# Convolution with per-token taps, then a two-layer SoLU network: other first loads, weights on two queues, and a new table of step priorities

## The chip, the core and the metric

The kernel runs on one core of a Trainium2 chip. The metric is device time in microseconds (us) of one execution. The five engines of the core are named as the profile names them: PE is TensorE (matmuls), DVE is VectorE, ACT is ScalarE, POOL is GpSimd, and SP is SyncE, which issues most of the DMAs. Each engine works through its own instructions in the order in which they were built; between engines they wait for each other with semaphores. A DMA is issued from an engine's queue (here SP's, after the change also ACT's) and moved by 16 DMA engines.

## The reference

Eight sequences of 4160 tokens of 192 channels pass through two stages. Cut to what is computed:

```python
w = softmax(weight_gen, axis=-1)              # 8 heads x 7 taps for every token
x_pad = concatenate([zeros(B, 6, D), x])      # six zero rows ahead of each sequence
out[s, h, :] = sum_k w[s, h, k] * x_pad[s + k, h, :]     # 24 channels a head
h = out @ w_in                                # 33280 x 192 times 192 x 1024
solu = h * softmax(h)
ln = (solu - mean) / sqrt(var + 1e-6) * g_ln
return ln @ w_out                             # 1024 x 192
```

Each token needs the six rows ahead of it in its own sequence; the first rows of a sequence need zeros there. The weights `w_in`, `w_out` and `g_ln`: the two matrices arrive as 64-bit floats, which the kernel reads as pairs of 32-bit integers and converts on the chip.

## The kernel before

The 33280 tokens are cut into 128 runs of 260 consecutive tokens, one run to a partition, 16 runs to a sequence. A "tile" t is the t-th token of all 128 runs, so there are 260 tiles. The tiles come in chunks (4, 8, 8 and then 16 tiles) for the loads and the softmax of the taps, and in groups of 4 (the first two groups have 2) for the convolution.

**First loads.** For chunk 0, `load_x(0)` needs the six rows ahead of each run. Those of run p are the last six rows of run p-1, except where a sequence begins (partitions 0, 16, 32, ...), where they are zeros. Before, one DMA brings them for partitions 1 to 127 at once (L78), wrongly also for the sequence starts, and a third DMA then writes zeros over these eight partitions from a small tile (L80). It has to wait until the first one has landed. All loads are issued from SP's queue in the order of the program: taps of chunk 0 (`load_w(0)`, L96), the last 64 rows of `w_in` (L152, tile `raw_b`, which the profile calls `hl` after its buffer), `load_x(0)` (L78 to L80), the first 128 rows of `w_in` in two halves (L168, `raw_a`), the taps of chunk 1, `w_out` (L173, `raw_2`, shown as `raw`), `g_ln` (L177), and `load_x(1)`. Each DMA reports its end through one of eight counters, which the program takes in turn (DMAHW0 to DMAHW7); a DMA that gets a counter again waits until the one that had it before has landed.

**Convolution.** POOL multiplies a group's rows by the taps (L133) and adds the seven products in two steps (L139, L141, into one of two `half` buffers). DVE does the last addition (L366, step `fin`, tile `a`), ACT copies some columns (L372, `dup`). The softmax of a chunk's taps is seven steps `t0` to `t6` on DVE (L112, L120, L124), POOL (L114, L126) and ACT (L118, L122).

**Network.** For each pair of tiles PE transposes (`xT`, L383) and ACT and DVE split the result into a high and a low part. For each tile then: the first product into one of three PSUM buffers `h` (`mm1`, L422 and L427), the negative maximum on DVE (`max`, L441), the exponential on ACT (`exp`, L454), SoLU on DVE (`solu`, L460), the sum of squares on ACT (`sq`, L466), the high half of the result on ACT (`hi`, L473), the low half on DVE (`lo`, L477), a DMA transpose (`tr`, L485), the second product into the single PSUM buffer `po` (`mm2`, L529), and the scaling by ACT (`out`, L540). The next `mm2` waits for this `out`, and a new `mm1` waits until the `sq` and `lo` of three tiles earlier have freed its buffer.

**Weights.** The conversion runs in seven parts of three steps: `b`, `a0`, `a1` for `w_in` (512 columns each, L194 to L213) and `c0` to `c3` for `w_out` (384 columns each). They use the PSUM buffers of `h` as scratch, so the first products wait for some of them.

**What sets the order.** `issue_order` is a planner that runs when the kernel is built. It has a table of steps with an assumed cost, an engine and what each step waits for, and plays them through: whenever an engine is free it takes, of the steps that could start, the one with the lowest `t + URGENCY[name]`. The order in which the steps start in this play is the order in which they are written to the engines' queues. `URGENCY` is a table of 90 numbers.

Of the kernel before, what the change touches and what calls it, by code (L numbers as in the profile page):

```python
# [26 lines left out]
def tile_kernel(ctx: ExitStack, tc: tile.TileContext, x, weight_gen, w_in, w_out, g_ln, out):  # L27
    nc = tc.nc
# [38 lines left out]
    def load_x(c, part=0):  # L67
        t0, n = starts[c], starts[c + 1] - starts[c]
        if part == 0:
            xs[c] = io.tile([P, (TC + HALO) * D], F32, name="xt")  # L70
        xt = xs[c]
        xv = xt.rearrange("p (t d) -> p t d", d=D)
        if c == 0:

            nc.gpsimd.memset(xt[:1, : HALO * D], 0.0)
# [2 lines left out]
            nc.sync.dma_start(xv[1:, :HALO, :], x_run[: P - 1, RUN - HALO :, :])  # L78
            nc.sync.dma_start(xv[:, HALO : HALO + n, :], x_run[:, :n, :])
            nc.sync.dma_start(  # L80
                xv[::PB, :HALO, :], zeros.unsqueeze(1).broadcast_to([B, HALO, D])
            )
# [82 lines left out]

    raw_a = att.tile([P, 2 * FF], I32, name="raw_a", bufs=1)
    for f in range(2):
        nc.sync.dma_start(  # L168
            raw_a[:, f * FF : (f + 1) * FF], w_in[:P, f * FF : (f + 1) * FF]
        )  # L170
    load_w(1)
    raw_2 = att.tile([P, 2 * NJ * D], I32, name="raw_2", bufs=1)
    nc.sync.dma_start(  # L173
        raw_2.rearrange("p (j d) -> p j d", j=NJ), w_out.rearrange("(j p) d -> p j d", p=P)
    )
    g = const.tile([P, NJ], F32, name="g")
    nc.sync.dma_start(g, g_ln.rearrange("(j p) -> p j", p=P))  # L177
    load_x(1)
# [81 lines left out]
    def scale_and_sum(f, step):  # L260
# [24 lines left out]
    def prepare_second(step, half=None):  # L285
# [307 lines left out]
    f5=-90.9, f6=-122.6, f7=-80.2, fin=-1.8, hi=21.6, lo=-147.6, lw=-22, lx0=-1.4, lx1=-11.2,
    lx2=-124.2, lx3=169.4, max=5.1, mm1=26.4, mm2=33.4, od=-130.9, out=-6, p30=-16.2, p31=3.9,
    p4=42.9, p5=103.1, p6=5.8, p70=-62.9, p71=0.3, p80=126.7, p81=-54.7, q00=-14.5, q01=-183.5,
    q02=-5.9, q10=-13.7, q11=-25.1, q12=-13.9, q20=-2.5, q21=-143.1, q22=-168.3, q30=-15.9,
    q31=149.2, q32=-18.4, solu=-21.3, sq=207.5, t0=45.9, t1=-70.9, t2=79, t3=26.5, t4=120.9,
    t5=135.7, t6=73.4, tr=65.6, vb=-74.8, vr=-11.3, xT=25.4, xhi=-202.9, xld=-11.7, xlo=-60.8,
    xn=7.8,
# [243 lines left out]
```

## Time and profile before

| | |
|---|---|
| time, median of 3 runs (lowest to highest) | 1389.33 us (1389.17 to 1389.57) |
| the profiled execution | 1389.4 us |
| its span, first to last instruction | 1387.5 us |
| busy: PE, DVE, ACT, POOL | 1259.2, 1230.0, 1128.5, 1247.0 us |
| granted clock of TensorE, mean | 0.991 |
| POOL's first multiplication of a group starts, its last addition ends | 31.59 us, 1288.46 us |

The span is counted from the first instruction; the remaining 1.9 us of the execution lie around it. In the timeline a row has the start, the duration, the engine, the source line, the operation and its tiles, and in brackets how long the engine had been idle and what released it; `SPq` rows are the issuing of a DMA, not its transfer. A row of stretches has the limits, the length, then the busy time of PE, weight loads, DVE, ACT and POOL with their counts, the granted clock, the busy share of the 16 DMA engines, and GB/s.

### The profile page before, as it was taken

The numbers are of one execution on the slowest core, as the hardware profiler recorded it, in microseconds if no ns is written. First come the engines' busy times: TensorE is split into PE (matmuls) and PEld (weight loads), VectorE is DVE, ScalarE is ACT, GpSimd is POOL, SyncE is SP. The second block draws the span as 40 slices with busy tenths as digits, with TensorE's granted clock in tenths as the row PEclk, the third lists the DMA queues.
The fourth block names the chain that finished last, engine by engine and source line by source line (L and its number), as shares of the span: only waits on it lengthen the run. The fifth ranks groups of instructions, "written<-read, shape, count | busy, mean of one in ns | idle before, by whom it ended". The sixth has DMA issues, their size and how long they took to land.

```text
span 1387.5 us, 26562 instructions
## 1 busy us (share of the span) xinstructions
PE 1259.2 (91%) x10028; PEld 988.6 (71%) x10028; DVE 1230.0 (89%) x2068; ACT 1128.5 (81%) x2231; POOL 1247.0 (90%) x243
## 2 busy tenths in 40 slices
PE   0389899999999999989989999999999999999997
PEld 0267677777777777767767677777777777777776
DVE  2999898999989899889989898989899889999984
ACT  1588887888888888888888888888788888888885
POOL 1999999999999999999999999999999999999100
PEclk9989999999999999999999999999999999999999
DMA  3469768696968789697857768687858668766765
GB/s 90 139 142 194 147 128 201 124 207 122 194 130 174 146 145 195 122 198 123 186 130 166 158 149 186 118 190 145 193 109 191 146 140 176 132 133 117 134 131 116
DMA packets 565241, 210.43 MB, mean 152 GB/s; under 512 B 544329, under 2 KB 545785, under 8 KB 565112
## 3 DMA queue, kind: packets, MB, share of 16 engines
q1 hardware_dynamic: 565112, 208.73, 72.5%
q8 instruction: 79, 1.29, 0.4%
q14 instruction: 50, 0.41, 0.1%
HBM read 46.19 MB, written 25.56 MB: 52 GB/s over the span
## 4 chain that ended last, share of the span: by engine, by line
POOL 51%; DVE 16%; issue 13%; ACT 13%; PE 4%; DMA 3%; SPq 0%; POOLq 0%; DVEq 0%; ACTq 0%
POOL pr L133 27%; POOL pr L139 15%; POOL half L141 6%; DVE h L460 5%; ACT hl L473 4%; DVE hl L477 4%; ACT e L466 3%; DVE stats L441 3%; ACT e L454 3%; DVE a L366 3%; DMA xt<-in_x_dram 2%; POOL wt L114 2%; PE po L529 2%; POOL wt L126 1%; PE h L422 1%
## 5 line engine op out<-in xcount | busy, mean ns | idle before, releaser
L133 POOL TENSOR_TENSOR pr<-xt,wt 128x5376 f32<-128x5376 f32 (+1 forms) x66 | 631.3, 9565 | 23.1 <-DMA xt<-zeros 20.5
L529 PE MATMUL po<-w_hl,hlT 128*128 128x192 f16 x6192 | 558.5, 247 | 26.6 <-ACT ot L540 26.2
L529 PEld LDWEIGHTS <-hlT 128*128 128x128 f16 x6240 | 515.2, 98 | 82.2 <-issue 79.2
L477 DVE SCALAR_TENSOR_TENSOR hl<-h,hl 128x1024 f16<-128x1024 f32 x260 | 315.4, 1220 | 44.2 <-ACT e L466 31.5
L460 DVE SCALAR_TENSOR_TENSOR h<-h,stats,e 128x1024 f32<-128x1024 f32 x260 | 334.7, 1288 | 22.4 <-ACT e L454 9.2
L473 ACT ACTIVATE hl<-h 128x1024 f16<-128x1024 f32 x260 | 267.3, 1028 | 92.3 <-DVE stats L497 57.4
L139 POOL TENSOR_TENSOR pr<-pr 128x2304 f32<-128x2304 f32 (+1 forms) x66 | 332.7, 5041 | 5.2
L441 DVE TENSOR_REDUCE stats<-h 128x1 f32<-128x1024 f32 x260 | 316.1, 1216 | 8.9 <-PE h L427 8.1
L454 ACT ACTIVATE e<-h,stats 128x1024 f32<-128x1024 f32 x260 | 292.6, 1126 | 31.1 <-DVE stats L441 27.2
L466 ACT ACTIVATE e<-h,stats 128x1024 f32<-128x1024 f32 x260 | 292.3, 1125 | 5.9 <-DVE hl L477 5.4
L422 PE MATMUL h<-wa_hi,x_hi 128*128 128x512 f32 x520 | 225.4, 433 | 36.3 <-ACT e L466 22.8
L141 POOL TENSOR_TENSOR half<-pr 128x1536 f32<-128x1536 f32 (+1 forms) x66 | 225.8, 3422 | 5.2
L422 PE MATMUL h<-wa_hi,x_lo 128*128 128x512 f32 x520 | 207.5, 399 | 0.8 <-ACT x_lo L405 0.8
L422 PE MATMUL h<-wa_lo,x_hi 128*128 128x512 f32 x520 | 206.3, 397 | 0.0
L422 PEld LDWEIGHTS h<-wa_hi,x_hi 128*128 128x128 f32 x520 | 98.9, 190 | 59.3 <-ACT e L466 26.0
L427 PE MATMUL h<-wb_hi,x_hi 64*128 64x512 f32 x520 | 131.1, 500 | 0.0
L383 PE MATMUL pa<-ident,a 128*128 128x128 f32 x520 | 84.6, 286 | 44.2 <-DVE a L366 44.1
L540 ACT ACTIVATE ot<-po,stats 128x192 f32<-128x192 f32 x258 | 111.4, 432 | 8.5 <-PE po L529 8.5
L366 DVE TENSOR_REDUCE a<-half 128x768 f32<-128x1536 f32 (+1 forms) x66 | 116.4, 1764 | 1.6 <-POOL half L141 1.6
L427 PEld LDWEIGHTS h<-wb_hi,x_hi 64*128 64x128 f32 x520 | 48.6, 184 | 96.7 <-issue 96.7
L422 PEld LDWEIGHTS h<-wa_hi,x_lo 128*128 128x128 f32 x520 | 98.6, 190 | 24.3 <-ACT x_lo L405 1.6
L383 PEld LDWEIGHTS pa<-ident,a 128*128 128x128 f32 x520 | 55.8, 142 | 79.7 <-DVE a L366 44.1
(79 smaller groups left out, 1194.1 us busy)
## 6 DMA issues: line engine op xcount, KB each, us to landing
out_dram<-ot SPq DMA_DIRECT2D x65, 384.0 KB, 3.3
xt<-in_x_dram SPq DMA_DIRECT2D x30, 576.0 KB, 4.7
xt<-in_x_dram SPq DMA_DIRECT2D x30, 480.0 KB, 4.7
wt<-in_weight_gen_dram SPq DMA_DIRECT2D x15, 448.0 KB, 4.1
hlT<-hl SPq DMA_TRANSPOSE x260, 4.5
raw<-in_moe_w_out_dram SPq DMA_DIRECT2D x1, 1536.0 KB, 9.4
xt<-in_x_dram SPq DMA_DIRECT2D x3, 384.0 KB, 6.0
raw_a<-in_moe_w_in_dram SPq DMA_DIRECT2D x2, 512.0 KB, 11.5
```

The source lines that it names most:

```text
L133: nc.gpsimd.tensor_tensor(out=window(pr, 0, [(TG * D, K), (HG, n * H), (1, HG)]), in0=window(xt, t * D, [(D, K), (HG, n * H), (1, HG)]), i ...
L139: nc.gpsimd.tensor_tensor(out=pr[:, :3], in0=pr[:, :3], in1=pr[:, 3:6], op=ALU.add)
L141: nc.gpsimd.tensor_tensor(out=half, in0=window(pr, 0, [(2 * TG * D, 2), (D, n), (1, D)]), in1=window(pr, TG * D, [(5 * TG * D, 2), (D, n), ...
L422: nc.tensor.matmul(h[:, fs], lhs[:, 0, :], rhs[:, fs], start=n == 0, stop=False)
L427: nc.tensor.matmul(h[:, fs], lhs[rows, 1, :], rhs[rows], start=False, stop=n == 2,)
L441: nc.vector.tensor_reduce(stat(t, NMAX), h_of[t], axis=AX.X, op=ALU.max, negate=True)
L454: nc.scalar.activation(e, h_of[t], AF.Exp, bias=stat(t, NMAX), accum_out=stat(t, Z))
L460: nc.vector.scalar_tensor_tensor(out=h, in0=h, scalar=stat(t, SIGMA), in1=e, op0=ALU.mult, op1=ALU.mult, accum_out=stat(t, M))
L466: nc.scalar.activation(e_of.pop(t), h_of[t], AF.Square, bias=stat(t, M), scale=-float(FF), accum_out=stat(t, Q),)
L473: nc.scalar.activation(hl[:, 0, :], h_of[t], AF.Copy, scale=2.0**14)
L477: nc.vector.scalar_tensor_tensor(out=hl[:, 1, :], in0=h_of[t], scalar=2.0**14, in1=hl[:, 0, :], op0=ALU.mult, op1=ALU.subtract,)
L529: nc.tensor.matmul(po[:, :D], hlT[:, half * NJ + j, :], w2_hl[:, j, w, :], start=n == 0, stop=n == len(terms) - 1,)
```

## The change

Four things change.

1. `load_x(0)`: POOL zeroes the six rows ahead on all 128 partitions first. Then eight DMAs, one for each sequence, load the rows for the 15 partitions behind its first one, the odd ones from SP's queue and the even ones from ACT's. The DMA that wrote zeros, and its tile, are gone.
2. The loads are issued in another order: `load_x(0)` directly after the first taps, and `raw_a`, the second half of `w_out` and `g_ln` from ACT's queue. All stand ahead of ACT's first work.
3. Two scratch tiles get a pool of their own (`frac` instead of a buffer of `e`), and the sums of squares of the second weights (`second["total"]`) take the upper half of the `po` buffer instead of `pa`.
4. The planner gets another `URGENCY` table, other assumed costs for some steps (POOL's convolution 14990 + 3510 ns instead of 14206 + 3380, for example), the part `a0` ahead of `b`, and a wait of the first scaling steps for `a02` and `a12`. No instruction of a tile is added or removed by this; they are put in another order.

```diff
-            nc.gpsimd.memset(xt[:1, : HALO * D], 0.0)
-            zeros = const.tile([B, D], F32, name="zeros")
-            nc.gpsimd.memset(zeros, 0.0)
-            nc.sync.dma_start(xv[1:, :HALO, :], x_run[: P - 1, RUN - HALO :, :])
+            nc.gpsimd.memset(xt[:, : HALO * D], 0.0)
             nc.sync.dma_start(xv[:, HALO : HALO + n, :], x_run[:, :n, :])
-            nc.sync.dma_start(
-                xv[::PB, :HALO, :], zeros.unsqueeze(1).broadcast_to([B, HALO, D])
-            )
+            for b in range(B):
+                queue = nc.sync if b % 2 else nc.scalar
+                queue.dma_start(
+                    xv[b * PB + 1 : (b + 1) * PB, :HALO, :],
+                    x_run[b * PB : (b + 1) * PB - 1, RUN - HALO :, :],
+                )
...
     load_w(0)
     w_in = w_in.bitcast(I32)
     w_out = w_out.bitcast(I32)
+    load_x(0)
+    raw_a = att.tile([P, 2 * FF], I32, name="raw_a", bufs=1)
 
     raw_b = big.tile([P, FF], I32, name="hl", bufs=3)
     for f in range(2):
+        nc.scalar.dma_start(raw_a[:, f * FF : (f + 1) * FF], w_in[:P, f * FF : (f + 1) * FF])
         nc.sync.dma_start(raw_b[f * D2 : (f + 1) * D2, :], w_in[P:, f * FF : (f + 1) * FF])
-    load_x(0)
+    load_w(1)
+    raw_2 = att.tile([P, 2 * NJ * D], I32, name="raw_2", bufs=1)
+    raw_2v = raw_2.rearrange("p (j d) -> p j d", j=NJ)
+    for n in range(2):
+        js = slice(n * NJ // 2, (n + 1) * NJ // 2)
+        (nc.scalar if n else nc.sync).dma_start(
+            raw_2v[:, js], w_out.rearrange("(j p) d -> p j d", p=P)[:, js]
+        )
+    g = const.tile([P, NJ], F32, name="g")
+    nc.scalar.dma_start(g, g_ln.rearrange("(j p) -> p j", p=P))
+    load_x(1)
...
-            frac = big.tile([P, FF], F32, name="e")[:, :n]
+            frac = big.tile([P, FH], F32, name="frac")[:, :n]
...
-            second["total"] = ps_a.tile([P, 512], F32, name="pa")
+            second["total"] = second["sums"][:, 256:]
...
-    c01=19.2, c02=4.8, c10=-143, c11=7.6, c12=1.7, c20=-15.4, c21=6.6, c22=-4.8, c30=-11.2,
-    c31=-125.2, c32=78.7, dup=-17.9, exp=66.3, f0=73.9, f1=1.2, f2=-140.6, f3=-73.6, f4=-146.4,
+    c31=12.4, c32=-106.7, dup=8.7, exp=-126.7, f0=126.6, f1=-167.6, f2=7.7, f3=-16.5, f4=2.1,
+    f5=-0.2, f6=-129.7, f7=-140.1, fin=-6.2, hi=27.1, lo=-2, lw=157.1, lx0=-8.4, lx1=-95.6,
...
-        add("attA", t, POOL, 14206 if full else 7302, *after, ready=21100 if c == 1 else 0)
-        add("attB", t, POOL, 3380 if full else 1764, ("attA", t), ("fin", groups[i - 2] if i > 1 else -1))
+        add("attA", t, POOL, 14990 if full else 7500, *after, ready=15000 if c == 1 else 9000)
+        add("attB", t, POOL, 3510 if full else 1800, ("attA", t), ("fin", groups[i - 2] if i > 1 else -1))
...
-        add("mm1", t, PE, 2300, low_of(t), ("sq", t - 3), ("lo", t - 3), *after)
+        add("mm1", t, PE, 2460, low_of(t), ("sq", t - 3), ("lo", t - 3), *after)
```

What this makes of the engines' queues is shown at three places. The first is the start of SP's queue before the change, with the counter that each DMA has to wait for (`Pool` is POOL's own counter; `raw_107` is the tile of `w_out`):

```order
L96 DMA wt<-in_weight_gen_dram 128x224
L152 DMA hl<-in_moe_w_in_dram 64x1024 x2
L78 DMA xt<-in_x_dram 127x1152
L79 DMA xt<-in_x_dram 128x768
L168 DMA raw_a<-in_moe_w_in_dram 128x1024
L80 DMA xt<-zeros 8x6x192 [waits DMAHW3_49,Pool_49]
L168 DMA raw_a<-in_moe_w_in_dram 128x1024
L96 DMA wt<-in_weight_gen_dram 128x448 [waits DMAHW0_49]
L173 DMA raw_107<-in_moe_w_out_dram 128x8x384 [waits DMAHW1_49]
L177 DMA g<-in_moe_g_ln_dram 128x8x1 [waits DMAHW2_49]
L85 DMA xt<-in_x_dram 128x1536
```

DMAHW3 is the counter of the load of L78, so everything below L80 stands behind that load. After the change SP's queue begins so:

```order
L96 DMA wt<-in_weight_gen_dram 128x224
L76 DMA xt<-in_x_dram 128x768
L79 DMA xt<-in_x_dram 15x1152 [waits Pool_49]
L79 DMA xt<-in_x_dram 15x1152 x2
L79 DMA xt<-in_x_dram 15x1152 [waits DMAHW1_49]
L155 DMA hl<-in_moe_w_in_dram 64x1024 [waits DMAHW3_49]
L155 DMA hl<-in_moe_w_in_dram 64x1024 [waits DMAHW5_49]
L96 DMA wt<-in_weight_gen_dram 128x448 [waits DMAHW7_49]
L161 DMA raw_101<-in_moe_w_out_dram 128x4x384 [waits DMAHW0_49]
L85 DMA xt<-in_x_dram 128x1536 [waits DMAHW2_49]
```

No DMA waits for a load of 127 rows any more, but nearly each waits for a counter. DMAHW0 belongs first to the taps of chunk 0, DMAHW1 to the load of L76, and DMAHW2 to DMAHW7 to the first six of the eight small loads. The start of ACT's queue after the change (before, its first two rows were the table load and the conversion that is L200 here):

```order
L56 ACT_TABLE_LOAD
L79 DMA xt<-in_x_dram 15x1152 [waits Pool_49]
L79 DMA xt<-in_x_dram 15x1152 x2
L79 DMA xt<-in_x_dram 15x1152 [waits DMAHW0_49]
L154 DMA raw_a<-in_moe_w_in_dram 128x1024 [waits DMAHW2_49]
L154 DMA raw_a<-in_moe_w_in_dram 128x1024 [waits DMAHW4_49]
L161 DMA raw_101<-in_moe_w_out_dram 128x4x384 [waits DMAHW6_49]
L165 DMA g<-in_moe_g_ln_dram 128x8x1 [waits DMAHW1_49]
L118 ACTIVATE wt<-wt 128x224 [waits Pool_49]
L200 ACTIVATE h<-h 128x512 [waits DVE_49]
```

The taps of chunk 0 (L118) now stand behind eight DMAs, the last of which waits for DMAHW1, whose second owner is the eighth small load. The second place is DVE's queue up to the division of the taps of chunk 0 (L124), after the change:

```order
L112 TENSOR_REDUCE wm<-wt 128x32 [waits DMAHW0_49]
L177 TENSOR_SCALAR minus<-ident 128x128 [waits Pool_49]
L193 TENSOR_SCALAR h<-raw_a 128x512 [waits DMAHW2_49]
L196 TENSOR_SCALAR h<-raw_a 128x512 [waits DVE_49]
L198 TENSOR_SCALAR h<-h 128x512 [waits DVE_49]
L193 TENSOR_SCALAR h<-hl 128x512 [waits DMAHW5_49,DMAHW3_49]
L196 TENSOR_SCALAR h<-hl 128x512 [waits DVE_49]
L120 TENSOR_REDUCE wm<-wt 128x32 [waits Activation_49]
L198 TENSOR_SCALAR h<-h 128x512 [waits DVE_49]
L112 TENSOR_REDUCE wm<-wt 128x64 [waits DMAHW7_49]
L124 RECIPROCAL wy<-wy 128x32 [waits Activation_49]
```

Before, the first conversion of `raw_b` (`hl`) stood directly behind the maximum of the taps, and the two tap steps of L120 and L124 ahead of any step on `raw_a`. The third place is the end of the convolution on DVE, the last addition of the last group (`a<-half`, tiles 256 to 259). Before:

```order
L441 TENSOR_REDUCE stats<-h 128x1
L477 SCALAR_TENSOR_TENSOR hl<-h,hl 128x1024
L445 TENSOR_REDUCE stats<-stats 128x1
L412 TENSOR_TENSOR x_lo<-pa,x_hi 128x512
L450 RECIPROCAL stats<-stats 128x1
L366 TENSOR_REDUCE a<-half 128x4x192
L497 TENSOR_REDUCE stats<-stats 128x4
L460 SCALAR_TENSOR_TENSOR h,stats<-h,stats,e 128x1024
```

Now (lines are one lower):

```order
L440 TENSOR_REDUCE stats<-h 128x1
L476 SCALAR_TENSOR_TENSOR hl<-h,hl 128x1024
L444 TENSOR_REDUCE stats<-stats 128x1
L496 TENSOR_REDUCE stats<-stats 128x4
L365 TENSOR_REDUCE a<-half 128x4x192
L496 TENSOR_REDUCE stats<-stats 128x4
L449 RECIPROCAL stats<-stats 128x1
L459 SCALAR_TENSOR_TENSOR h,stats<-h,stats,e 128x1024
```

The neighbours are alike; what moved is the place. In DVE's queue before, 244 of the 260 `solu` steps stand ahead of this last addition and 16 behind it; now 249 stand ahead and 11 behind. At the addition for the group that begins with tile 52 it was 48 and is 49, at tile 152 it was 144 and is 148.

More of the change, by code (lines that the diff above doesn't have):

```diff
@@ L164, in tile_kernel @@
     nc.vector.tensor_scalar_mul(minus, ident, -1.0)
[L166 to L178, printed above, removed]
     for step in range(TAP_STEPS):
@@ L278, in scale_and_sum @@
         elif step == 2:
-            junk = big.tile([P, FF], F32, name="e")
+            junk = big.tile([P, FH], F32, name="frac")
             nc.scalar.activation(
@@ L588 @@
 URGENCY = dict(
-    a00=-79.4, a01=-110.4, a02=-10.4, a03=-9.5, a04=28.3, a10=35.2, a11=8.2, a12=-10.4, a13=2,
-    a14=-26.4, attA=14.7, attB=-118.7, b0=12.5, b1=28.4, b2=-7.8, b3=-40.9, b4=125.7, c00=120.1,
-    c01=19.2, c02=4.8, c10=-143, c11=7.6, c12=1.7, c20=-15.4, c21=6.6, c22=-4.8, c30=-11.2,
-    c31=-125.2, c32=78.7, dup=-17.9, exp=66.3, f0=73.9, f1=1.2, f2=-140.6, f3=-73.6, f4=-146.4,
[L593 to L599, printed above, removed]
+    a00=146.3, a01=114, a02=105.5, a03=52.4, a04=58.5, a10=-4.3, a11=-0.8, a12=-8.4, a13=73.8,
+    a14=25.5, attA=-2.8, attB=-19.6, b0=129.4, b1=-57.8, b2=-0.3, b3=52.7, b4=-112.9, c00=44.6,
+    c01=2.8, c02=-91.1, c10=-93.1, c11=-37.1, c12=-89.4, c20=-34.5, c21=-4.7, c22=16.6, c30=-144.9,
+    c31=12.4, c32=-106.7, dup=8.7, exp=-126.7, f0=126.6, f1=-167.6, f2=7.7, f3=-16.5, f4=2.1,
+    f5=-0.2, f6=-129.7, f7=-140.1, fin=-6.2, hi=27.1, lo=-2, lw=157.1, lx0=-8.4, lx1=-95.6,
+    lx2=125.7, lx3=8.5, max=40, mm1=26.6, mm2=33.6, od=-17.4, out=4.8, p30=-113.1, p31=-64.5,
+    p4=-117.2, p5=143.6, p6=-0.8, p70=179.3, p71=-15.2, p80=-6.7, p81=15.1, q00=3.8, q01=-15.7,
+    q02=16.8, q10=-99.3, q11=-14.1, q12=5, q20=-108.4, q21=-65.1, q22=0.2, q30=110, q31=144.7,
+    q32=51.3, solu=-130.8, sq=374, t0=10.4, t1=3.2, t2=84, t3=121.1, t4=-15.6, t5=26.9, t6=2.8,
+    tr=-113, vb=-142.7, vr=-62.5, xT=24.7, xhi=-12, xld=-20.5, xlo=3.7, xn=-4.4,
 )
@@ L620, in once @@
         add(name, 0, engine, cost, *((x, 0) for x in after), ready=ready)
-    parts = ["b", "a0", "a1", *(f"c{f}" for f in range(4))]
+    parts = ["a0", "b", "a1", *(f"c{f}" for f in range(4))]
     for n, part in enumerate(parts):
         w_in, size = n < 3, 512 if n < 3 else 384
-        at = (5600, 9000, 10600)[n] if w_in else 16200
+        at = (9000, 10500, 12000)[n] if w_in else 15000
         before = () if w_in else (f"{parts[n - 3]}4" if n < 6 else "q00",)
@@ L637, in issue_order @@
             f = n - 3
-            once(f"q{f}0", ACT, 700, part + "2")
+            once(f"q{f}0", ACT, 700, part + "2", "a02", "a12")
             once(f"q{f}1", PE, 660, f"q{f}0", *([f"q{f - 1}1"] if f else []))
@@ L704, in issue_order @@
     for t in range(0, run, 2):
-        add("xT", t, PE, 600, ("dup", group_of[t]), low_of(t - 2))
+        add("xT", t, PE, 500, ("dup", group_of[t]), low_of(t - 2))
         add("xhi", t, ACT, 478, ("xT", t), ("mm1", t - 3))
         if on_vector(t):
-            add("xld", t, DVE, 560, ("xhi", t), ("mm1", t - 3))
+            add("xld", t, DVE, 600, ("xhi", t), ("mm1", t - 3))
         else:
@@ L719, in issue_order @@
             after.append(("p80" if t == 3 else "p81", 0))
-        add("mm1", t, PE, 2300, low_of(t), ("sq", t - 3), ("lo", t - 3), *after)
-        add("max", t, DVE, 1131, ("mm1", t), ("exp", t - 4))
+        add("mm1", t, PE, 2460, low_of(t), ("sq", t - 3), ("lo", t - 3), *after)
+        add("max", t, DVE, 1140, ("mm1", t), ("exp", t - 4))
         add("vb", t, DVE, 70, ("max", t), ("f7", stats_of[t - 24] if t >= 24 else -1))
@@ L724, in issue_order @@
         add("exp", t, ACT, 1091, ("max", t), ("sq", t - 2))
-        add("solu", t, DVE, 1210, ("exp", t), ("vr", t))
+        add("solu", t, DVE, 1290, ("exp", t), ("vr", t))
         add("sq", t, ACT, 1091, ("solu", t))
-        add("hi", t, ACT, 904, ("solu", t), ("tr", t - 3))
+        add("hi", t, ACT, 920, ("solu", t), ("tr", t - 3))
         add("lo", t, DVE, 1135, ("hi", t))
@@ L734, in issue_order @@
             after.append(("out", t - 1))
-        add("mm2", t, PE, 2200, ("tr", t), *after)
+        add("mm2", t, PE, 2170, ("tr", t), *after)
         add("out", t, ACT, 304, ("mm2", t), ("f7", stats_of[t]), ("od", t // 4 * 4 - 5))
```

4 lines of the change are left out of this document (2 added, 2 removed).

## The prediction

> **What bounds the kernel now.** I read the page first, then the busy time by stretches, cut where POOL's convolution begins and ends.
>
> ```profile
> span 1387.5 us, 26562 instructions
> POOL 51%; DVE 16%; issue 13%; ACT 13%; PE 4%; DMA 3%; SPq 0%; POOLq 0%; DVEq 0%; ACTq 0%
> ...
> 0.00:31.59 31.59, 0.00 (x0) 0.00 (x0) 4.01 (x9) 2.97 (x5) 3.10 (x11) 1.00 0.25 74
> 31.59:1288.50 1256.91, 1168.95 (x9264) 915.15 (x9265) 1153.87 (x1933) 1052.67 (x2081) 1243.85 (x232) 0.99 0.75 156
> 1288.50:1387.50 99.00, 90.21 (x767) 73.44 (x765) 72.15 (x128) 72.85 (x147) 0.00 (x0) 0.98 0.65 124
> ```
>
> There are three stages. In the first 31.59 us no engine does more than 4 us of work. In the second POOL is busy 1243.85 of 1256.91 us, which is all but the gaps between its instructions; the chain of waits goes half through POOL. In the last 99 us POOL has nothing left and PE works off a backlog. Next, what fills the first stage, from the timeline:
>
> ```profile
> 2.46 0.48 SPq L78 DMA_DIRECT2D xt<-in_x_dram  x1
> 2.99 9.88 SPq L79 DMA_DIRECT2D xt<-in_x_dram  x1
> 12.92 1.37 SPq L168 DMA_DIRECT2D raw_a<-in_moe_w_in_dram  x1
> 28.82 0.75 SPq L80 DMA_DIRECT2D xt<-zeros  x1
> ...
> 31.08 0.69 DVE L194 TENSOR_SCALAR h<-raw_a 128x512 int32<-128x512 int32 x1 [20.61 <-DMA raw_a<-in_moe_w_in_dram]
> 31.59 4.95 POOL L133 TENSOR_TENSOR pr<-xt,wt 128x2688 f32<-128x2688 f32 x1 [20.46 <-DMA xt<-zeros]
> ```
> ```profile
> 20.00:28.00 8.00, 0.00 (x0) 0.00 (x0) 0.00 (x0) 0.00 (x0) 0.00 (x0) 1.00 0.06 26
> ```
>
> The zeros (L80) are issued at 28.82, when the load of the 127 rows (L78) has landed; POOL waits 20.46 us for them, DVE 20.61 us for weights. From 20 to 28 us the 16 DMA engines are busy 0.06 of the time, one sixteenth: that load runs on one of them.
>
> What sets the pace afterwards is read from `solu` on DVE, with two records for each tile, and from its rows around the last group:
>
> ```profile
> 200.00:600.00 400.00, 106.77 (x160) 1.00 0.79 160
> 600.00:1000.00 400.00, 106.16 (x158) 1.00 0.77 160
> 1000.00:1288.50 288.50, 78.07 (x116) 0.99 0.70 144
> ```
> ```profile
> 64.72 1.28 DVE L460 SCALAR_TENSOR_TENSOR h<-h,stats,e 128x1024 f32<-128x1024 f32 x1
> ...
> 1295.12 1.79 DVE L366 TENSOR_REDUCE a<-half 128x768 f32<-128x1536 f32 x1
> ...
> 1296.90 1.29 DVE L460 SCALAR_TENSOR_TENSOR h<-h,stats,e 128x1024 f32<-128x1024 f32 x1
> ...
> 1368.74 1.28 DVE L460 SCALAR_TENSOR_TENSOR h<-h,stats,e 128x1024 f32<-128x1024 f32 x1
> ```
>
> That is 217 tiles in 1088.5 us, 5.02 us a tile. After the last group's addition, 16 tiles follow with 15 steps in 71.84 us, 4.79 a tile, then 17.5 us of drain. POOL needs 1256.91/260 = 4.83 a tile. So the loop over PE, DVE and ACT is slower than POOL by 0.19 us a tile, and its backlog is the last 99 us. Both begin late for the same reason.
>
> **The change part by part.** *The rows ahead of a run.* Durations for the new loads:
>
> ```profile
> 0.73 1.05 POOL L75 MEMSET xt<- 1x1152 f32 x1 [0.29 <-POOLq L823]
> 0.73 1.28 ACT L56 ACT_TABLE_LOAD   x1 [0.73 <-PEq L823]
> 0.74 0.41 SPq L96 DMA_DIRECT2D wt<-in_weight_gen_dram  x1
> 1.93 0.20 POOL masks.py:197 MEMSET ident<- 128x128 f32 x1
> 2.78 0.39 DVE L112 TENSOR_REDUCE wm<-wt 128x32 f32<-128x224 f32 x1 [1.78 <-DMA wt<-in_weight_gen_dram]
> ```
> ```profile
> xt<-in_x_dram SPq DMA_DIRECT2D x30, 480.0 KB, 4.7
> raw_a<-in_moe_w_in_dram SPq DMA_DIRECT2D x2, 512.0 KB, 11.5
> ...
> hl<-in_moe_w_in_dram SPq DMA_DIRECT2D x2, 256.0 KB, 3.6
> ```
>
> The memset grows from 1 to 128 partitions at equal length; 128 elements on 128 partitions take 0.20 us, so I keep 1.05, ending at 1.78. The removed DMA and its memset of 8 partitions free only time that nobody waited for. Issues take about 0.45 us and a small load lands in 2.04 (0.74 to 2.78). ACT, after its table load, issues its first small load at 2.01, which lands at 4.1; its fourth waits for the first taps (2.78), no delay. SP's fourth waits for the rows of L76 (384 KB, issued at 1.2; 3.6 to 4.7, so 4.8 to 5.9) and lands by 8. So the rows are there at about 8 instead of 31.59, if a load of 15 rows runs on several engines. Below: on one engine.
>
> The Trainium skill, page "DMA: Bandwidth & Descriptors", section "Why a DMA increments its semaphore by 16 and not by 1", says that the largest number up to 16 that divides the slowest dimension gives the engines: 1 for 127 rows, which the 0.06 above bears out, and 15 for 15 rows, which no run here shows. By it, eight descriptors queue on an engine and the sum stands.
>
> *ACT's queue.* All eight DMAs stand ahead of its first work. `raw_a` waits for the first small load (4.1) and takes, by the other loads, 3.6 to 4.7: 7.7 to 8.8, I take 8.2. `g` waits for the eighth small load (8), so the exponential of the taps starts at about 8.6, and DVE, which has conversions ahead of its use, comes to it later still (below): no loss. Behind it on ACT stand the conversions, which wait for DVE anyway.
>
> The Trainium skill, the same page, section "Issuing engines are not separate DMA queues", speaks against a gain in bandwidth from ACT's queue: all queues share the 16 engines, and only issue time is saved. By it, as in my sum, the second queue by itself brings nothing.
>
> *DVE up to the first multiplication.* The new order puts five conversions ahead of the sum of the taps:
>
> ```profile
> 5.73 0.70 DVE L194 TENSOR_SCALAR h<-hl 128x512 int32<-128x512 int32 x1 [2.56 <-DMA hl<-in_moe_w_in_dram]
> ...
> 10.12 0.35 DVE L124 RECIPROCAL wy<-wy 128x32 f32<-128x32 f32 x1 [0.30 <-ACT wy L122]
> 10.55 0.57 POOL L126 TENSOR_TENSOR wt<-wt,wy 128x224 f32<-128x224 f32 x1 [6.73 <-DVE wy L124]
> ...
> 39.90 0.61 DVE L112 TENSOR_REDUCE wm<-wt 128x64 f32<-128x448 f32 x1
> 41.08 0.97 POOL L114 TENSOR_TENSOR wt<-wt,wm 128x448 f32<-128x448 f32 x1
> 43.07 0.96 DVE L366 TENSOR_REDUCE a<-half 128x384 f32<-128x768 f32 x1
> ```
>
> A conversion takes 0.7: five from 8.2 end at 11.7; then the sum of the taps (as long as their maximum, 0.39), a conversion, L112 (0.61) and the reciprocal (0.35) end at 13.8; POOL's L126 takes 0.57. The first multiplication starts at about 14.5: 17.1 us earlier. The first group ends 9.5 later (31.59 to 41.08), at 24.0. DVE by then has its 13 further steps of 0.7 done (13.8 + 9.1 = 22.9), so the first addition starts at 24.1 instead of 43.07, 19.0 earlier. The loop behind it (second weights, first products) moves along; its first `mm1` waits for conversions on DVE, which follow that addition in both orders.
>
> Bounds: without the conversions ahead of the taps POOL would start at about 11 (8.6 and the tap steps). If `raw_a` took 11.5 us to land, as on the page (there it stood behind the 127 rows), POOL would start at 21.9, a gain of 9.7. I take 14.5, nearest to loads that stand behind nothing.
>
> The scratch tiles and the `po` half change no instruction, only what waits at the start, in the cover of DVE's conversions; without it, some tenths.
>
> *The new order.* Nothing is added, so its price is in the waits. DVE's queue has 11 tiles left behind the last addition instead of 16. If POOL's end set the end, five tiles of 4.79, 24 us, would go from the last stage; if the loop keeps 5.02, nothing. For all of it the loop must pass 249 tiles between its start, now 64.72 - 19.0 = 45.7, and about 1276, or 4.94 a tile. What an order could remove:
>
> ```profile
> DVE a L366 <- POOL half L141: 1.6, 3, 0.8
> PE po L529 <- ACT ot L540: 26.2, 30, 3.1
> PE h L422 <- ACT e L466: 22.8, 12, 9.1
> PE pa L398 <- ACT x_hi L391: 10.4, 18, 2.4
> PE h L422 <- DVE hl L477: 9.3, 12, 1.5
> ```
>
> DVE hardly waits for POOL (1.6 us), so the loop's own waits count: on PE 68.7 us in 72 waits. The bounds are a gain of 24 and a loss of the same size. 24 would take a third of these waits, while PE is already busy 93% of the stage. I take a third of 24, 8 us.
>
> *Sum* against the profiled execution (1389.4, of which 1.9 lie around the span; the runs' median is 1389.33): 1389.4 - 19.0 - 8 = 1362.4, rounded to 1363.
>
> **The rivals.** *The start alone (27%).* The new order gives nothing: 1389.4 - 19.0 = 1370.4. For it: 5.02 a tile is what PE, DVE and ACT reach together, and they are busy 93, 92 and 84% of the stage. Against: the largest waits are those of order.
>
> *POOL sets the end (15%).* The loop reaches 4.94. POOL ends 17.1 earlier, at 1271.4; the last addition ends some 5 us later, 1276; from there to the end it was 1387.5 - 1296.9 = 90.6, now less 24, so 1343 and with the 1.9 around it 1345. For it: 4.79 without the additions. Against: PE's 1168.95 + 90.21 us over 260 tiles are 4.84 a tile, so it asks 98% of PE.
>
> *The loads don't spread (5%).* The eight loads of 15 rows run on one engine, one after the other: 120 rows at the pace of the 127 (2.46 to 28.82, 0.21 us a row) from 2.0 on land at 27. POOL gains about 4, and ACT's `raw_a` is stuck too: 1385. For it: the stretch at 0.06. Against: that it was so for 127 rows says little of 15.
>
> *Slower (5%).* `out` gives way to `exp`. In ACT's queue `out` stands directly behind an `exp` 110 times before and 158 times now, and PE waits for it before the next `mm2`.
>
> ```profile
> L454 ACT ACTIVATE e<-h,stats x260: 1096/1118/1217, 62.3 to 1367.5; 128x1024 f32<-128x1024 f32 x130
> L454 ACT ACTIVATION_READ_ACCUMULATOR e<-h,stats x260: 185/206/308, 63.3 to 1368.5; 128x1 f32 x130
> ```
>
> An `exp` with its read is 1.32 us; 48 bare ones cost 63 us, 1433 in all with the start's gain. It decides from 17 bare ones (22 us). Against: an `mm1`, longer than an `exp`, mostly lies between two `mm2`.
>
> **How the numbers follow.** The forecast has 45% (1352 to 1367), the others 27, 15, 5 and 5, and 3% go to a start that gains only 9.7 (1380). The range 1345 to 1375 holds the first three and leaves out some 18%. The median of three runs can tell 0.2% (2.8 us) from no change. Faster by more: 45 + 27 + 15, and 6 of the 8 where little of the start is left: 93%; within 0.2%: the other 2%; slower: 5%.
>
> **What would show it.** Right: the first multiplication at 13 to 16 us and the first addition at 22 to 26; no single-engine stretch; `solu` below 5.0 us a tile; POOL's last addition near 1271 and some 11 tiles behind it. Wrong: a DMA share of 0.06 while POOL waits; ACT's L118 after 12 us; a wait of PE for `ot` well over 26 us; `solu` at 5.02 or more.

## The result, and the profile after

The changed kernel takes 1351.49 us (median of 4 runs, 1350.31 to 1351.77) against 1389.25 us before (4 runs, 1389.12 to 1389.57): a ratio of 0.9726, with a 95% interval of 0.9709 to 0.9743. The forecast was 1363, in a range of 1345 to 1375. The profiled execution took 1351.8 us, its span is 1350.0. Of the changed kernel, the page's span and chain, and the stretches, again cut where POOL's convolution begins and ends:

```profile
span 1350.0 us, 26629 instructions
DVE 31%; ACT 23%; POOL 19%; issue 15%; PE 9%; DMA 2%; ACTq 0%; SPq 0%; DVEq 0%; POOLq 0%
...
0.00:17.99 17.99, 0.00 (x0) 0.00 (x0) 6.43 (x14) 4.23 (x7) 2.94 (x11) 1.00 0.85 251
17.99:1278.36 1260.37, 1192.16 (x9480) 936.04 (x9480) 1172.42 (x1969) 1068.17 (x2123) 1244.34 (x232) 0.99 0.76 156
1278.36:1350.00 71.64, 63.32 (x552) 52.27 (x548) 48.84 (x87) 50.97 (x102) 0.00 (x1) 0.96 0.65 124
```

The first stage is shorter by 13.6 us (31.59 to 17.99), POOL's stage is longer by 3.5 (1256.9 to 1260.4), and what stands behind it is shorter by 27.4 (99.0 to 71.6). Together that is the 37.5 us between the spans. So more went behind POOL's end than at the start. Most of the 3.5 us is one new wait of POOL for DVE (a row of waits has the total in us, the times, the longest):

```profile
POOL wt L114 <- DVE stats L449: 3.0, 1, 3.0
```

The start, from the timeline and the DMA issues (size, then median time to landing):

```profile
1.82 1.90 ACTq L79 DMA_DIRECT2D xt<-in_x_dram  x4
6.25 0.91 ACTq L154 DMA_DIRECT2D raw_a<-in_moe_w_in_dram  x2
8.80 0.39 ACT L118 ACTIVATE wt<-wt 128x224 f32<-128x224 f32 x1 [6.79 <-DMA xt<-in_x_dram]
12.11 0.69 DVE L193 TENSOR_SCALAR h<-raw_a 128x512 int32<-128x512 int32 x1 [8.76 <-DMA raw_a<-in_moe_w_in_dram]
17.33 0.58 POOL L126 TENSOR_TENSOR wt<-wt,wy 128x224 f32<-128x224 f32 x1 [13.46 <-DVE wy L124]
17.99 4.95 POOL L133 TENSOR_TENSOR pr<-xt,wt 128x2688 f32<-128x2688 f32 x1
...
27.55 0.96 DVE L365 TENSOR_REDUCE a<-half 128x384 f32<-128x768 f32 x1 [1.50 <-POOL half L141]
```
```profile
raw_a<-in_moe_w_in_dram ACTq DMA_DIRECT2D x2, 512.0 KB, 6.8
...
xt<-in_x_dram SPq DMA_DIRECT2D x4, 67.5 KB, 4.1
xt<-in_x_dram ACTq DMA_DIRECT2D x4, 67.5 KB, 4.4
```

DVE waits for `raw_a` until 12.11, not 8.2. The small loads on ACT's queue, on the first of which `raw_a` waits, took 4.4 us (median) where 2.04 were put in, so `raw_a` is issued at 6.25 instead of 4.1. Its first half, the one DVE waits for, then takes 5.9 us to land where 4.1 were put in; the 6.8 is the median of both halves. The pace, from the stretches of `solu` (two records a tile), and the last group's addition:

```profile
200.00:600.00 400.00, 108.98 (x162) 1.00 0.79 166
600.00:1000.00 400.00, 110.10 (x164) 1.00 0.80 164
1000.00:1278.36 278.36, 76.85 (x115) 1.00 0.75 146
```
```profile
1281.96 1.78 DVE L365 TENSOR_REDUCE a<-half 128x768 f32<-128x1536 f32 x1
```

These are 220.5 tiles in 1078.36 us, 4.89 a tile instead of 5.02. The last addition starts 3.6 us after POOL's end, before 6.7.

### The profile page after: what moved, and what is told of

It is laid out like the page before. It is cut to its first block, busy times and chain, and to the rows that moved or that the text cites. A ratio compares the mean times of both kernels' runs of the same rounds, so it can differ in the third digit from the quotient of the medians.

```text
span 1350.0 us, 26629 instructions
## 1 busy us (share of the span) xinstructions
PE 1255.5 (93%) x10028; PEld 988.3 (73%) x10028; DVE 1227.7 (91%) x2068; ACT 1123.4 (83%) x2231; POOL 1247.3 (92%) x242
## 4 chain that ended last, share of the span: by engine, by line
DVE 31%; ACT 23%; POOL 19%; issue 15%; PE 9%; DMA 2%; ACTq 0%; SPq 0%; DVEq 0%; POOLq 0%
POOL pr L133 10%; DVE h L459 10%; ACT hl L472 7%; DVE hl L476 7%; ACT e L465 7%; DVE stats L440 7%; POOL pr L139 6%; ACT e L453 5%; PE po L528 4%; DVE a L365 3%; PE h L421 3%; POOL half L141 2%; PE h L426 2%; ACT ot L539 1%; DVE x_lo L411 1%
## 5 line engine op out<-in xcount | busy, mean ns | idle before, releaser
L528 PE MATMUL po<-w_hl,hlT 128*128 128x192 f16 x6192 | 557.9, 247 | 24.2 <-ACT ot L539 22.9
L421 PEld LDWEIGHTS h<-wa_lo,x_hi 128*128 128x128 f32 x520 | 99.5, 191 | 11.8
```

Of the source, the lines that this page charges most:

```text
L421: nc.tensor.matmul(h[:, fs], lhs[:, 0, :], rhs[:, fs], start=n == 0, stop=False)
L528: nc.tensor.matmul(po[:, :D], hlT[:, half * NJ + j, :], w2_hl[:, j, w, :], start=n == 0, stop=n == len(terms) - 1,)
```

## The experiments

Each kernel was timed against the kernel before in the same session; its ratio and interval are given. The table has what the profiles of all of them show: the start of POOL's first multiplication, the end of its last addition, the span, what lies between the two last, and how many `solu` stand behind DVE's last addition.

| kernel | first multiplication | POOL's end | span | behind POOL | tiles behind |
|---|---|---|---|---|---|
| before | 31.59 | 1288.46 | 1387.5 | 99.0 | 16 |
| changed | 17.99 | 1278.36 | 1350.0 | 71.6 | 11 |
| loads_only | 16.73 | 1274.14 | 1373.3 | 99.2 | 16 |
| order_only | 31.52 | 1293.03 | 1363.5 | 70.5 | 11 |
| rows_split | 11.76 | 1271.41 | 1369.7 | 98.3 | 16 |
| one_load | 38.64 | 1299.26 | 1371.1 | 71.8 | 11 |
| before_pool_less | 31.77 | 1263.25 | 1361.1 | 97.9 | 16 |
| pool_less | 18.18 | 1267.25 | 1340.6 | 73.4 | 11 |
| old_costs | 16.72 | 1273.84 | 1373.7 | 99.9 | 16 |
| old_urgency | 18.04 | 1289.71 | 1372.1 | 82.4 | 13 |
| split_new_order | 10.91 | 1273.53 | 1344.2 | 70.7 | 11 |
| weights_first | 14.19 | 1275.31 | 1346.9 | 71.6 | 11 |
| one_queue | 7.95 | 1276.05 | 1346.5 | 70.5 | 11 |
| split_less_pool | 11.10 | 1265.86 | 1339.4 | 73.5 | 11 |

**The two halves apart.** First the kernel before with the new first loads only (points 1 and 2 of the change), then the changed kernel with the first loads of before (points 3 and 4 only).

```diff
-            nc.sync.dma_start(xv[1:, :HALO, :], x_run[: P - 1, RUN - HALO :, :])
+            for b in range(B):
+                queue = nc.sync if b % 2 else nc.scalar
...
+        nc.scalar.dma_start(raw_a[:, f * FF : (f + 1) * FF], w_in[:P, f * FF : (f + 1) * FF])
```

> The kernel before with the new first loads alone (the rows ahead of a run in eight loads, half of the weights on ACT's queue), old table and old costs. Theory A, the two halves of the change add: the first addition moves from 43.07 us to some 27.5, as in the changed kernel, the loop keeps its 5.02 us a tile and 16 tiles stay behind the last addition, so 1389.3 - 15 = 1374. Theory B, the early start is lost again in the first twenty tiles, as 10 of the changed kernel's 15 us were (tile 20's solu ended 5 us earlier there, not 15): 1384.

Measured: 1375.17 us, 0.9900 (0.9886 to 0.9915), 14.2 us less than before.

```diff
-        add("attA", t, POOL, 14206 if full else 7302, *after, ready=21100 if c == 1 else 0)
+        add("attA", t, POOL, 14990 if full else 7500, *after, ready=15000 if c == 1 else 9000)
...
-    c31=-125.2, c32=78.7, dup=-17.9, exp=66.3, f0=73.9, f1=1.2, f2=-140.6, f3=-73.6, f4=-146.4,
+    c31=12.4, c32=-106.7, dup=8.7, exp=-126.7, f0=126.6, f1=-167.6, f2=7.7, f3=-16.5, f4=2.1,
```

> The changed kernel with the old first loads: new table, new costs, scratch tiles as in the change, rows ahead of a run by one load of 127 rows and zeros behind it. POOL's first multiplication stays at about 31.6 us. Theory A, the halves add: 4.88 us a tile as in the changed kernel, 11 tiles behind the last addition, 1389.3 - 23 = 1366. Theory B, POOL sets the end in the new order and the loop has only to keep up with it: POOL ends at 1288.5 to 1292, and 72 us behind it 1362. Theory C, the new order pays only together with the early loads: above 1380.

Measured: 1365.30 us, 0.9827 (0.9813 to 0.9842), 24.1 us less. The halves add, 38.3 against the 37.8 of the whole. In the table the first half moves the first two columns and leaves 99 us behind POOL. The second leaves the start and makes 70.5 of the 99, which is 28.5 less, but POOL ends 4.6 us later (1293.03 against 1288.46). The scratch tiles (point 3) are part of this half and were not tried alone; `old_costs` below keeps them and gains nothing over `loads_only`.

**The load of 127 rows.** In the kernel before, only this load is cut in two:

```diff
-            nc.sync.dma_start(xv[1:, :HALO, :], x_run[: P - 1, RUN - HALO :, :])
+            for r0, r1 in ((1, 113), (113, P)):
+                nc.sync.dma_start(xv[r0:r1, :HALO, :], x_run[r0 - 1 : r1 - 1, RUN - HALO :, :])
```

> The kernel before with a single edit: the load of 127 rows is cut into one of 112 and one of 15 rows, all else as before (zeros behind them, SP's queue). If 127 rows sat on one DMA engine because of their number, the rows land within some 5 us, the zeros are issued at 8 to 10 instead of 28.82, the first multiplication comes at 12 to 16, and with the order of before 1389.3 - 15 to 19 = 1370 to 1374. If something else held the load back (its place in the queue, the reading of other runs' rows), nothing changes: 1389.

Measured: 1371.19 us, 0.9871 (0.9855 to 0.9888). This one edit gains 18 us, more than the 14.2 that all the new first loads of the change gain with the order of before. Its issues and stretch:

```profile
2.46 1.11 SPq L79 DMA_DIRECT2D xt<-in_x_dram  x2
3.61 0.36 SPq L80 DMA_DIRECT2D xt<-in_x_dram  x1
8.94 0.76 SPq L81 DMA_DIRECT2D xt<-zeros  x1
```
```profile
2.00:9.00 7.00, 0.00 (x0) 0.00 (x0) 2.60 (x5) 0.91 (x3) 1.06 (x4) 1.00 0.86 227
```

The zeros are issued at 8.94, not 28.82. The DMA engines are busy 0.86 of the stretch, where before there was a long one at 0.06. By the DMA issues of this run the 112 rows (504 KB) landed in 6.4 us and the 15 rows in 6.0, where the 127 took 26.4. So it is the number of rows that put the load on one engine. The rule of the Trainium skill, page "DMA: Bandwidth & Descriptors", section "Why a DMA increments its semaphore by 16 and not by 1", agrees: the number of engines is the largest up to 16 that divides the rows, so 1 for 127 rows, 16 for 112 and 15 for 15. The run shows that both parts spread, not over how many engines.

The other way round: the changed kernel with one load of 127 rows in the place of its eight. The zeros at the starts of seven sequences are left out: the first tokens there take rows of the sequence ahead.

```diff
-            for b in range(B):
-                queue = nc.sync if b % 2 else nc.scalar
-                queue.dma_start(
-                    xv[b * PB + 1 : (b + 1) * PB, :HALO, :],
-                    x_run[b * PB : (b + 1) * PB - 1, RUN - HALO :, :],
-                )
+            nc.sync.dma_start(xv[1:, :HALO, :], x_run[: P - 1, RUN - HALO :, :])
```

> The changed kernel with the eight loads put back into one of 127 rows on SP's queue; the zeros at the starts of seven sequences are left out, so their first tokens take rows of the sequence ahead. The load takes some 24 us, POOL's first multiplication comes at about 27 to 29 instead of 17.99; the weights, on ACT's queue, are not held back. If POOL sets the end of the changed kernel: 1351.5 + 10 = 1362, with the same 72 us behind POOL's last addition. If the loop sets it, it has weights early and catches up with the groups later: 1352 to 1356.

Measured: 1371.90 us, 0.9875 (0.9860 to 0.9889). The multiplication starts at 38.64, ten us later than expected, since the load holds up its queue, too, and with it the weights in `hl`:

```profile
1.82 0.30 SPq L77 DMA_DIRECT2D xt<-in_x_dram  x1
2.16 15.86 SPq L150 DMA_DIRECT2D hl<-in_moe_w_in_dram  x2
...
36.08 0.69 DVE L188 TENSOR_SCALAR h<-hl 128x512 int32<-128x512 int32 x1 [27.97 <-DMA hl<-in_moe_w_in_dram]
```

Two issues that take 1.2 us in the changed kernel take 15.86 behind it. The start is 20.65 us later than in the changed kernel, POOL's end 20.9, the span 21.1: the delay goes through to the end in full. But the expectation's two theories are not parted by it. The weights came as late as the rows, and the first `mm1` starts at 62.58 us instead of 41.67, so the loop lost the same 20.9 us as POOL.

**Does the loop set the pace, or POOL?** POOL loses 17 of its instructions (L114, the subtraction of the taps' maximum, for all chunks but the first; the softmax is the same up to rounding), 28 us, in the kernel before and in the changed one:

```diff
-        elif step == 1:
+        elif step == 1 and c == 0:
             nc.gpsimd.tensor_tensor(
                 out=w3, in0=w3, in1=m.unsqueeze(2).broadcast_to(wide), op=ALU.subtract
             )
```

> The same edit on the kernel before: 28 us less for POOL, all queues otherwise as before. The prediction held that the loop sets the pace there (5.02 us a tile against POOL's 4.83): then nothing changes, 1389. If the order ties the loop to POOL and POOL sets the pace: POOL ends some 25 us earlier with 16 tiles and 99 us behind it, 1364.

Measured: 1363.28 us, 0.9811 (0.9794 to 0.9827), 26.6 us less. The 5.02 us a tile were not the loop's own:

```profile
200.00:600.00 400.00, 110.46 (x164) 1.00 0.81 168
600.00:1000.00 400.00, 107.53 (x160) 1.00 0.77 160
```
```profile
DVE a L366 <- POOL half L141: 11.5, 12, 1.5
```

162 tiles in 800 us are 4.94 a tile with the same instructions in the same order on DVE, ACT and PE. The prediction's reading of the kernel before falls with this run. Even now the loop waits for POOL: DVE's wait for POOL's additions, 1.6 us in 3 waits before, has become 11.5 in 12.

> The changed kernel without POOL's subtraction of the maximum from the taps (L114) for all chunks but the first; the softmax is the same up to rounding. Nothing else moves in any queue. POOL has 17 instructions less, 28 us of its 1247. Theory A, POOL sets the pace and the end: POOL's last addition comes some 25 us earlier and so does the end, 1325. Theory B, the loop over PE, DVE and ACT has its own 4.88 us a tile and POOL only happens to keep level: the end stays within 3 us of 1351.5 and POOL waits for its buffers. PE's busy time, 1255 us, bounds the gain.

Measured: 1342.95 us, 0.9663 (0.9649 to 0.9678), 8.5 us less than the changed kernel: between the two theories. POOL ends 11.1 us earlier, not 25, since it now waits, most of it for DVE and ACT to come to its next taps:

```profile
POOL wt L126 <- DVE wy L124: 13.6, 1, 13.6
POOL wt L126 <- ACT stats L499: 5.5, 1, 5.5
POOL wt L126 <- ACT stats L515: 4.5, 1, 4.5
POOL wt L126 <- DVE stats L444: 4.2, 1, 4.2
POOL wt L126 <- ACT ot L539: 2.3, 1, 2.3
```

(The 13.6 are the start.) So POOL still counts in the changed kernel, but with some 9 us less of it the loop is what POOL waits for.

**How POOL held the loop.** A wait on ACT, which the prediction did not look at, carries POOL's pace to the loop. Its row in the kernel before, in the changed one, and in `old_costs` below:

```profile
ACT wt L118 <- POOL wt L114: 39.6, 15, 4.5
```
```profile
ACT wt L118 <- POOL wt L114: 13.8, 6, 6.5
```
```profile
ACT wt L118 <- POOL wt L114: 33.6, 15, 4.6
```

In `old_urgency` below it is:

```profile
ACT wt L118 <- POOL wt L114: 17.6, 11, 4.5
```

In the kernel before, in 13 of the 15 long chunks and in two short ones, ACT comes to the exponential of the taps (L118) before POOL has done the subtraction, and stands for 2.6 us on average, with `exp`, `sq`, `hi` and `out` of the tiles queued behind it. How far the loop goes in step with POOL is seen from these exponentials: the time from that of the fifth long chunk to that of the fifteenth, ten chunks, and the tiles whose `solu` ran in it.

| kernel | ten long chunks, us | tiles in them |
|---|---|---|
| before | 773.3 | 153 |
| loads_only | 773.7 | 153 |
| old_costs | 773.5 | 153 |
| old_urgency | 773.5 | 156.5 |
| order_only | 774.1 | 158.5 |
| changed | 773.0 | 158.5 |
| before_pool_less | 754.4 | 152.5 |
| pool_less | 772.9 | 158.5 |

Ten chunks of 16 tiles at POOL's 4.83 us are 773 us. So the loop of the kernel before goes in step with POOL, and its order has 153 tiles in the time in which POOL does 160: that is the slow pace of some 5 us a tile. The new order has 158.5 tiles in the same time, 5.5 more, about the five that no longer stand behind the last addition. With 28 us less on POOL the kernel before does its tiles of these chunks in 19 us less. The changed kernel does not: at 4.88 us a tile its loop is then at its own limit, and its gain of 8.5 us is won ahead of this stretch, where its fifth long chunk comes 8.0 us earlier (292.53 against 300.57).

What becomes of ACT's wait is told by the two halves of point 4 of the change: the changed kernel with the assumed costs and rules of before, and with the table of before.

```diff
-        add("attA", t, POOL, 14990 if full else 7500, *after, ready=15000 if c == 1 else 9000)
+        add("attA", t, POOL, 14206 if full else 7302, *after, ready=21100 if c == 1 else 0)
...
```

> The changed kernel with the assumed costs and rules of before, new table kept. 16 tiles stand behind the last addition in DVE's queue. Theory A: five tiles of 4.8 us more, 1351.5 + 24 = 1375. Theory B, the table alone brings the gain: 1352.

Measured: 1375.62 us, 0.9904 (0.9889 to 0.9919). With the old costs the planner writes the old relation of POOL to the loop with either table: 16 tiles behind, 15 waits of ACT, the time of `loads_only`.

```diff
-    c31=12.4, c32=-106.7, dup=8.7, exp=-126.7, f0=126.6, f1=-167.6, f2=7.7, f3=-16.5, f4=2.1,
+    c31=-125.2, c32=78.7, dup=-17.9, exp=66.3, f0=73.9, f1=1.2, f2=-140.6, f3=-73.6, f4=-146.4,
...
```

> The changed kernel with the table of before, new costs kept. In DVE's queue 13 tiles then stand behind the last group's addition, against 11 with both and 16 before. Theory A, POOL's work is passed through at its own pace and the number of tiles left behind it gives the end: two tiles of 4.8 us more, 1351.5 + 9.6 = 1361. Theory B, the gain is the table's, in waits it avoids: 1375, as with the loads alone.

Measured: 1373.94 us, 0.9890 (0.9875 to 0.9904). The time is near theory B's, the way to it is neither's alone: 82.4 us behind POOL's end, 10.8 more than with 11 tiles as theory A has it, and POOL ends 11.4 us later, because it waits:

```profile
POOL wt L126 <- DVE wy L124: 25.1, 3, 13.5
POOL wt L114 <- DVE stats L449: 2.8, 1, 2.8
```

Of the 25.1 us, 13.5 are the start; the rest are two stops of POOL, and with the one of L114 all three come before 115 us. Against `loads_only`, which has the old costs and the old table, 16.8 us less stand behind POOL's end, but that end comes 15.6 later. So with the old table the new costs take more than half of ACT's wait away (40.9 us in `loads_only`, 17.6 here) and put early stops on POOL instead; with the new table most of these stops are gone. Neither half is worth much without the other. That the loop goes in step with POOL is shown by the table above; that ACT's wait is what holds it is argued from these rows, not shown: the run that took L114 away removed the wait and the work on POOL together, and its loop still waited for POOL on DVE.

**What the start could still give.** Three variants. The new order with the old list of loads and the 127 rows cut, as in `rows_split`:

> The new order with the old list of first loads, in which the load of 127 rows is cut into 112 and 15 rows: all from SP's queue, the zeros behind them. If the start and the order add, as the first runs have it: POOL's first multiplication at about 11.8 us as with the split alone, some 6 us ahead of the changed kernel's 17.99, and POOL's end with 72 us behind it: 1345. If the first loads of the changed kernel are better by their second queue: above 1352.

Measured: 1346.68 us, 0.9693 (0.9678 to 0.9707), 4.8 us less than the changed kernel, with a single queue and the zeros as before. The first multiplication, at 10.91, waits 4.88 us for the zeros. Then `raw_a` ahead of the eight small loads:

```diff
+    for f in range(2):
+        nc.scalar.dma_start(raw_a[:, f * FF : (f + 1) * FF], w_in[:P, f * FF : (f + 1) * FF])
     load_x(0)
...
-                queue = nc.sync if b % 2 else nc.scalar
+                queue = nc.sync
```

> The changed kernel with the first rows of w_in issued from ACT's queue ahead of the eight small loads, which all go to SP's queue. If the first multiplication at 17.99 us was late because these weights landed at 12.1 us and DVE had to convert them ahead of the taps, they land by 7 now, and the first multiplication comes at 12 to 13, or where the eighth small load lands if that is later; the end follows by the same amount, 1346. If the small loads were the cause, all on one queue they come later, and the end stays or grows.

Measured: 1348.43 us, 0.9704 (0.9689 to 0.9718). The first multiplication moves from 17.99 to 14.19, and what it waits for last is now the rows (3.10 us); the end follows by 3.1 of the 3.8 us. Last, the changed kernel with all first loads on SP's queue:

```diff
-                queue = nc.sync if b % 2 else nc.scalar
+                queue = nc.sync
...
-        nc.scalar.dma_start(raw_a[:, f * FF : (f + 1) * FF], w_in[:P, f * FF : (f + 1) * FF])
+        nc.sync.dma_start(raw_a[:, f * FF : (f + 1) * FF], w_in[:P, f * FF : (f + 1) * FF])
...
-        (nc.scalar if n else nc.sync).dma_start(
+        nc.sync.dma_start(
...
-    nc.scalar.dma_start(g, g_ln.rearrange("(j p) -> p j", p=P))
+    nc.sync.dma_start(g, g_ln.rearrange("(j p) -> p j", p=P))
```

> The changed kernel with all first loads on SP's queue, in the same order. If ACT's queue saves only issue time: eight issues of 0.45 us in a row, POOL's first multiplication 1 to 4 us later than 17.99, the end as much later, 1353 to 1356. If the second queue shares the engines better, more than that.

Measured: 1348.03 us, 0.9704 (0.9688 to 0.9720), 3.5 us less than with two queues where 1 to 4 more were expected. In this build the first taps also stand ahead of the conversions in DVE's queue, so this is not the queue alone. The multiplication starts 10.0 us earlier. Then POOL waits for the taps of chunk 1, which stand behind conversions in DVE's queue, and its third multiplication is 5.2 us earlier (33.75 against 38.94). A later wait for DVE, 5.9 us instead of 3.0, takes 2.9 more, and 2.3 us arrive at POOL's end:

```profile
4.96 0.35 DVE L124 RECIPROCAL wy<-wy 128x32 f32<-128x32 f32 x1 [0.29 <-ACT wy L122]
7.95 4.94 POOL L133 TENSOR_TENSOR pr<-xt,wt 128x2688 f32<-128x2688 f32 x1 [1.99 <-DMA xt<-in_x_dram]
...
19.18 0.97 POOL L114 TENSOR_TENSOR wt<-wt,wm 128x448 f32<-128x448 f32 x1 [1.72 <-DVE wm L112]
...
32.70 0.97 POOL L126 TENSOR_TENSOR wt<-wt,wy 128x448 f32<-128x448 f32 x1 [3.06 <-DVE wy L124]
33.75 9.70 POOL L133 TENSOR_TENSOR pr<-xt,wt 128x5376 f32<-128x5376 f32 x1
```
```profile
POOL wt L114 <- DVE stats L449: 5.9, 1, 5.9
```

The two edits that helped most, together (the loads of `split_new_order`, and POOL without L114):

> The two edits that helped, together: new order, the old list of first loads with 112 and 15 rows, and no subtraction of the maximum of the taps on POOL but in the first chunk. If the edits add: 1346.7 - 8.5 = 1338. If the loop is at its own limit already: 1342 to 1347.

Measured: 1341.32 us, 0.9659 (0.9645 to 0.9674). It has the lowest median of the study, 1.6 us below `pool_less`, though their intervals overlap. The two gains don't add: POOL starts 7 us earlier than in `pool_less` and ends 1.4 earlier, and waits the difference. It gives up the maximum in the softmax of the taps, which these inputs don't need but larger ones would. Of the kernels that keep it `split_new_order` has the lowest median; the intervals of `one_queue` and `weights_first` overlap with its own.

## Why the prediction was right, and where not

*The load of 127 rows on one DMA engine, and that loads of 15 rows spread:* right. `rows_split` shows the first, and the landing of the eight loads in 4.1 to 4.4 us with a share of 0.85 in the new first stage the second. The rival in which they don't spread is out.

*The start:* right in kind, mis-sized. The term "lands in 2.04" was taken from the load of the taps, which is issued first; the small loads took 4.1 to 4.4. From 1.82 to 6.25 us the DMA engines are busy 0.85 and move 219 GB/s, about the 924 KB of the eight small loads and of the rows of L76 together, so the small loads shared the engines with each other and with those rows. That put `raw_a` 2.15 us later, and its first half took 5.9 us to land instead of 4.1. The first multiplication came at 17.99, not 14.5. The gain was 13.6, not 17.1, and for the first addition 15.5 (43.07 to 27.55), not 19.0. The sum of the steps on DVE behind `raw_a` held: 5.9 us from 12.11 against 6.3 from 8.2. So did the exponential of the taps on ACT, 8.80 against 8.6.

*"The loop over PE, DVE and ACT is slower than POOL", and so "the loop's own waits count":* wrong. `before_pool_less` shows that the loop can go faster than 5.02 and that POOL's 28 us count almost fully. The pace was that of the order, 153 tiles in ten of POOL's chunks. A rate that is lower than POOL's does not show that the loop is the bound where its queues are tied to POOL's steps once in a chunk. A row that speaks against it, ACT's 39.6 us of waiting for POOL's L114, stands in the same view as the five rows quoted; only those of PE and DVE were read.

*The price of the new order:* the term "a third of 24" was too small. It measured 24.1 alone. That this is the whole of its bound is in part chance: 28.5 us went behind POOL's end, not 24, and POOL ended 4.6 later. The count in DVE's queue was the right thing to read for the last stage: 16, 13 and 11 tiles behind the last addition go with 98 to 100, 82 and 70 to 74 us.

*The rivals.* "POOL sets the end" (15%, 1345) is what happened: POOL's ten chunks take the 773 us they took before, and fewer tiles stand behind them. With the start and POOL's stage as they came, its own sum is 1387.5 - 13.6 + 3.5 - 24 = 1353.4, and some 3 more went because the last addition stood 3.6 instead of 6.7 us behind POOL; the span is 1350.0. That 1363 lay no further from the result than 11.5 us is in part luck: the sum took 19.0 for the start and 8 for the order, and alone they measured 14.2 and 24.1, so one error made up for some of the other. Its reason for the 8, that the loop keeps its own pace, is the step that failed. (1362.4 rounds to 1362, not 1363; nothing hangs on it.) Of its signs, the first multiplication (17.99, not 13 to 16), the first addition (27.55, not 22 to 26) and POOL's end (1278.36, not near 1271) missed; the pace, the 11 tiles and the absence of a stretch on one engine came as said. "The start alone" is out by `order_only`. The slower one, `out` behind `exp`, is out: PE's wait for `ot` is 22.9 us, below the 26.2 before.

```profile
PE po L528 <- ACT ot L539: 22.9, 36, 2.9
```

## What to carry to other kernels

Two engines that end a stage within a few per cent of each other are judged by taking work from one of them, not by comparing their rates: here 28 us less for POOL moved the end by 26.6 before the change and by 8.5 after it. Read the waits of every engine, the lightly loaded ones too, and look for the one that comes once in each chunk. Where an order is planned ahead, count in the queue of the next engine what is left behind the last step of the engine that ends first; that count times the pace is most of what follows that step (11 tiles of 4.89 are 54 of the 71.6 us, 16 of 5.02 are 80 of the 99.0). It is a price only as long as the step itself does not come later, as it did in `old_urgency`. Here assumed costs that were off by a few per cent (17.6 us for a group that takes 18.5) decided the count more than the priorities did: 16 tiles with the old costs and the new table, 13 with the new costs and the old table. The gain in time needed both.

## What the runs showed of the hardware

The load of 127 rows costs twice. It runs on one DMA engine (26.4 us, at a DMA share of 0.06), and it stops the queue behind it: one issue behind it took 9.88 us in the kernel before, two took 15.86 in `one_load`, against about 0.45 to 0.6 each otherwise. In `one_load` the two loads behind it then took 25.9 us to land (median), against 5.1 in the changed kernel. Eight loads of 15 rows and 67.5 KB took 4.1 to 4.4 us to land, twice the 2.1 of the first load, 112 KB on 128 partitions; they shared the engines with each other and with a load of 384 KB (a share of 0.85). Whether their few rows cost anything beyond that was not tried. The kernel with the second queue was not faster than the one with a single queue (1351.49 against 1348.03), but the order on DVE differed as well.
